# The first query chunk's attention scores as three 32-row products on four row strips

## The chip, the core and the metric

One core of a Trainium2 chip runs the kernel. The metric is device time in microseconds (us), median over executions. The core's engines work side by side: TensorE (PE; the profile shows its matmuls as PE and its weight loads as PEld), VectorE (DVE), ScalarE (ACT), GpSimd (POOL) and SyncE (SP). In this kernel POOL and SP mainly issue DMAs; those of SP are shown as SPq. TensorE writes its results to eight PSUM banks of 128 partitions by 512 fp32 values, from which ACT and DVE read.

## The reference

The output puts two results side by side: multi-query attention (A) of one `x`, and a two-dimensional Fourier filter (B) of another.

```python
# A: S = 2048, D = 448, H = 16 heads of 28, one key and one value head
q = (x @ wq).reshape(B, S, H, Dh).transpose(0, 2, 1, 3)
k, v = x @ wk, x @ wv
scores = einsum("bhqd,bkd->bhqk", q, k) * (Dh ** -0.5)
p = softmax(scores, axis=-1)
a = einsum("bhqk,bkd->bhqd", p, v).transpose(0, 2, 1, 3).reshape(B, S, H * Dh) @ wo
# B
y = irfft2(rfft2(x2) * (w_r + 1j * w_i), s=(S, D))
return concatenate([a, y], axis=-1)
```

## The kernel before, in words

**First part.** `x` is projected to queries, keys and values in fp32r (each operand split into a high part h and a low part l, three products hh + hl + lh). Beside this run the first transforms of B, all but the last of eight blocks. The order here is made by `Plan`: tasks with engines, durations and due times, put in order greedily. Queries lie in `qraw`: group g (four heads) and query chunk c (512 queries) make a 128 x 512 block, each head in a 32-row strip (28 values, then 4 rows that another use fills). The queries are masked and an upper bound for the scores is added in the spare rows (`cvec`), so that the exponential needs no maximum. A number `bits`, read by all engines, decides whether a rare branch (`tc.If`, L616) is taken; it is not taken here.

**Main part.** 256 steps: for c in 4 chunks, g in 4 groups, kc in 16 blocks of 128 keys. A step has:

- four scores (L1124), one for each head: a product of 128 rows, weights `ka[:, 128 keys]`, moving `qa[c, g][:, head]`. The 128 rows hold the key parts kh, kh, kl, kl in four strips and the query parts qh, ql, qh, ql, so that one product gives (kh + kl)(qh + ql). Each goes to one of banks 0 to 6;
- four exponentials on ACT (L1141), bank to `p` in SBUF, which free the bank;
- values (L1156): four 32-column products in fp32, one for each head, added up over the 16 key blocks of a group in bank 7. The profile counts each as two matmuls.

`build_q` makes `qa` of a group while the group before runs: three DVE operations (L195 to L197), then nine DMAs on SP (L206, L207) that put the head strips of qh and ql into the four strips of one of two slots. For the first group, L604, L606 and `twice` (L188) do the same with ACT and DVE copies at the end of the first part. `keys_cast`, `keys_low` and `keys_strip` (L484) make `ka`: the first half of the keys in the first part, the second half at the start of the main part.

After a group, `group_out` (L1001) copies bank 7 out, and it is normalised through POOL DMAs. After a chunk, 12 "w" units multiply by the output weights (`woh`, `wol`; L1044), and the last stages of B ("z" units L946, L972) fill TensorE too. `wo_load` and `wo_split` (L760, L763, L765) load and split the output weights. B's middle transforms run on DVE behind everything else.

**What sets the order.** The main part is written out by a planner. It keeps a clock for each engine (`clk`) with assumed costs and chooses on TensorE between scores, values and fill units; DVE work is queued by planned time (`after`, `background`). Every engine then executes its own list in order; the planned times never reach the chip. `size()` gives the steps of one batch of values: two, or four when enough fill work is there, so that TensorE changes between 128-row products and 32-column ones once in two or four steps. Fill units are allowed only where `work` holds them; in the first chunk there are none but one piece of B (`first_fill`).

Of the kernel before, what the change touches and what calls it, by code (L numbers as in the profile page):

```python
# [32 lines left out]
LEAD = 7  # L33
WARM = 8, 8
FIRST = 8
PLACES = (3, 5, 6, 8, 9, 10)


# [57 lines left out]
def kernel(ctx: ExitStack, tc: tile.TileContext, t: dict):  # L96
# [87 lines left out]

    qa, slots = {}, []

    def twice(u, q, *_):
        return nc.vector.tensor_copy(q[64:128, 2 * u:2 * u + 2], q[0:64, 2 * u:2 * u + 2].bitcast(F32))  # L188

    def build_q(c, g, first=False):  # L190
        cs = slice(c * CW, (c + 1) * CW)
        qt = qp.tile([128, CW], F32, name="qt")
        qh = qp.tile([128, CW], F32R, name="qh")
        ql = qp.tile([128, CW], F32R, name="ql")
        nc.vector.tensor_scalar(qt, qraw[:, g, cs], mask, cvec[:, g, c:c + 1], op0=ALU.mult, op1=ALU.add)  # L195
        nc.vector.tensor_copy(qh, qt)
        nc.vector.tensor_tensor(ql, qt, qh.bitcast(F32), op=ALU.subtract)  # L197
# [4 lines left out]
        if first:  # L202
            return q, qh, ql
# [8 lines left out]
    with tc.tile_pool(name="f1", bufs=2) as f1[0], tc.tile_pool(name="w1", bufs=1) as w1, ExitStack() as ctx1:  # L212
# [257 lines left out]
        kls, hi_ = {}, {}  # L470

        def keys_cast(h, eng):
            hs = slice(h * 1024, h * 1024 + 1024)
            cast(eng, lambda: ka[:32, hs], lambda: kf[:32, hs])

        def keys_low(h):
            hs = slice(h * 1024, h * 1024 + 1024)
            kls[h] = w1.tile([32, 1024], F32R, name="kl")
            low(lambda: kls[h], lambda: kf[:32, hs], lambda: ka[:32, hs])

        def keys_strip(h, p):
            hs = slice(h * 1024, h * 1024 + 1024)
            src = ka[0:32, hs] if p == 1 else kls[h]
            nc.sync.dma_start(ka[32 * p:32 * p + 32, hs].bitcast(F32), src.bitcast(F32))  # L484

        halves = slice(0, 1024), slice(1024, 2048)

# [33 lines left out]
        slots.append(qp.tile([128, 4, CW], F32R, name="qa0", bufs=1))  # L521
        qa[0, 0] = slots[0]

        for c in range(1, NC):
            for g in range(NG):
# [21 lines left out]
                if c == 2 and g == 3:  # L547
                    fetch("v", range(7, 14), slice(0, 1536), POOL, *(evacs[a, b] for a in range(3) for b in (1, 2, 3)))
                    kc = add(ACT, 1.0, lambda: keys_cast(0, ACT), krow_[0], *fetched["k0"])
                    kl = add(DVE, 1.1, lambda: keys_low(0), kc)  # L550
                    for p in (1, 2, 3):
                        add(SP, 0.55, lambda p=p: keys_strip(0, p), kl, kb=128)
# [45 lines left out]
        tv = add(PE, 1.05, turn_values, users[-6], ident_, *krow_, *fetched["v"])  # L598
        users.append(add(ACT, 0.6, lambda: nc.scalar.activation(vs, pvs[0], AF.Copy), tv))
        fm_task(L, True)  # L600
        cq = []
        for i in range(4):
            r = slice(32 * i, 32 * i + 32)
            cq.append([add(ACT, 0.6, lambda i=i, r=r: nc.scalar.activation(slots[0][32:64, i], q3[2][r].bitcast(F32), AF.Copy),  # L604
                           qd, due=56.0 + i),
                       add(DVE, 0.41, lambda i=i, r=r: nc.vector.tensor_copy(slots[0][0:32, i], q3[1][r].bitcast(F32)),  # L606
                           qd, due=56.0 + i)])
# [8 lines left out]
        with tc.If(rv > int(np.float32(BOUND).view(np.int32))), tc.tile_pool(name="g1", bufs=1) as g1:  # L616
# [24 lines left out]
            nc.vector.memset(cvec, 0.0)  # L641
            nc.vector.memset(mask, 1.0)
            parts = build_q(0, 0, True)
            q, qh, ql = parts
            for i in range(4):
                for p, src in enumerate((qh, ql)):
                    nc.vector.tensor_copy(q[32 * p:32 * p + 32, i], src[32 * i:32 * i + 32].bitcast(F32))
            for u in range(2):
                twice(u, q)


        fft1_out(L, pb6)
# [36 lines left out]
    def wide(n):  # L689
        return 0.165 + 0.00107 * n  # L690

    woh = ap.tile([128, 7, D], F32R, name="woh", bufs=1)
    wol = ap.tile([128, NG, D], F32R, name="wol", bufs=1)
    csh = ap.tile([128, 4, 128], F32R, name="csh", bufs=1)
    csl = ap.tile([128, 4, 128], F32R, name="csl", bufs=1)

# [63 lines left out]
        nc.gpsimd.dma_start(wo[g], t["wo"][:, g])  # L760

    def wo_split(g):
        V.tensor_copy(woh[:, g], wo[g])  # L763
        if g < NG:
            TT(wol[:, g], wo[g], woh[:, g].bitcast(F32), op=ALU.subtract)  # L765


    t1v = t1.rearrange("(r k) l u (n f) -> r (k l u) n f", r=2, f=113)
# [269 lines left out]
    def wo_mm(p, c, k, gs):  # L1038
        s = slice(k * 128, k * 128 + 128)
        for g in gs:  # L1040
            spare = c < NC - 1
            for n, (x, w, m) in enumerate(((oh, woh, g), (oh, wol, g), (ol, woh, g + 3 * spare))):
                if n < 2 or g or not spare:
                    mm(p, x[c][:, g, s], w[:, m], start=(g == 0 and n == 0), stop=(g == NG - 1 and n == 2))  # L1044

    def wo_out(p, c, k):
        y = ap.tile([128, D], F32, name="ya")
# [72 lines left out]
    def score(i):  # L1120
# [12 lines left out]
        if kc == 0 and h == 0 and n + 1 < len(order):  # L1133
            after(clk["pe"] + 3.0, 1.7, build_q, *order[n + 1])

    def exps():

        while waiting and waiting[0][0] < 4 * done_steps + P_BUFS:
            i, b, at = waiting.popleft()
            p = pt[i] = pp.tile([128, CW], F32, name="p")  # L1140
            nc.scalar.activation(p, bank[b], AF.Exp, scale=SCALE)  # L1141
# [45 lines left out]
    sc, bt, begun, since, gap = 0, 0, False, 0, 2  # L1187
    parts, tail = deque((k, g) for k in range(4) for g in range(NG - 1)), {}

    def partial():  # L1190
# [19 lines left out]
        return max(1.8, n * (total - done[0]) / max(250 - done_steps, 3)) if n > 2 else 0.0  # L1210

    done_steps, quota = 0, 0.0
    n = size()
    while done_steps < 256:
        if begun:
            vector(clk["pe"])
# [5 lines left out]
        if not begun and not soon:  # L1222
            first_fill()
            begun = True
        elif t_v <= clk["pe"] + 0.05 and (sc >= min(need + LEAD, 1024) or not soon):
            values(done_steps, n)
            done_steps += n
            exps()
# [171 lines left out]
```

## Time and profile before

| | |
|---|---|
| median of 3 runs | 634.85 us (634.68 to 637.08) |
| profiled execution | 635.8 us, its span 633.1 us |
| first score starts | 70.33 us |
| first exponential starts | 70.83 us |
| ACT in the stretch 71.43 to 196.52 us (chunk 0) | busy all of it, with 257 exponentials, the two cut by its ends counted |
| granted TensorE clock | 1.000 over the span |

Times in the rows are from the start of the span. A row of a timeline has start, length, engine, line, operation, output <- input, how many are merged, and in brackets how long the engine was idle before and what ended that. A matmul's length is from its start to its modelled end, so lengths of neighbours overlap; the pace is read from starts.

### The profile page before, as it was taken

The numbers are of one execution on the slowest core, as the hardware profiler recorded it, in microseconds if no ns is written. First come the engines' busy times: TensorE is split into PE (matmuls) and PEld (weight loads), VectorE is DVE, ScalarE is ACT, GpSimd is POOL, SyncE is SP. The second block draws the span as 40 slices with busy tenths as digits, with TensorE's granted clock in tenths as the row PEclk, the third lists the DMA queues.
The fourth block names the chain that finished last, engine by engine and source line by source line (L and its number), as shares of the span: only waits on it lengthen the run. The fifth ranks groups of instructions, "written<-read, shape, count | busy, mean of one in ns | idle before, by whom it ended". The sixth has DMA issues, their size and how long they took to land.

```text
span 633.1 us, 11646 instructions
## 1 busy us (share of the span) xinstructions
PE 626.6 (99%) x4336; PEld 351.5 (56%) x4336; DVE 347.3 (55%) x693; ACT 546.5 (86%) x1100; POOL 90.5 (14%) x167
## 2 busy tenths in 40 slices
PE   9999999999999999999999999999999999999997
PEld 7877544444444446554446656657564446564445
DVE  6999624979796988897632713236562201330104
ACT  4644899999999998789998788878779998879991
POOL 1021140102121101020223011021110101020200
PEclk9999999999999999999999999999999999999999
DMA  8766587031243231131763432251523121140002
GB/s 297 249 181 159 141 244 235 16 84 45 66 130 89 75 83 31 61 83 26 223 211 97 128 84 76 64 145 65 163 83 68 31 67 31 36 110 2 16 1 87
DMA packets 30738, 64.62 MB, mean 102 GB/s; under 512 B 7105, under 2 KB 16673, under 8 KB 29717
## 3 DMA queue, kind: packets, MB, share of 16 engines
q1 hardware_dynamic: 22714, 42.33, 23.8%
q0 software_dynamic: 7536, 20.98, 11.2%
q8 instruction: 34, 0.56, 0.4%
q10 hardware_dynamic: 432, 0.57, 0.2%
q14 instruction: 22, 0.18, 0.1%
HBM read 30.58 MB, written 16.30 MB: 74 GB/s over the span
## 4 chain that ended last, share of the span: by engine, by line
PE 88%; ACT 0%; issue 0%; DVE 0%; ACTq 0%
PE b L1124 41%; PE b L1156 37%; PE b L1044 5%; PE b L946 2%; PE b L972 2%; PE b L1277 0%; PE b L162 0%; ACT yb L1059 0%; DVE yb L1062 0%; ACTq L1060 0%
## 5 line engine op out<-in xcount | busy, mean ns | idle before, releaser
L1141 ACT ACTIVATE p<-b 128x512 f32<-128x512 f32 x1024 | 506.3, 769 | 40.9 <-PE b L1156 28.7
L1124 PE MATMUL b<-qa,ka 128*128 128x512 f32 x1024 | 282.7, 408 | 0.4 <-PEq L616 0.4
L1124 PEld LDWEIGHTS b<-qa,ka 128*128 128x128 f32 x1024 | 181.8, 188 | 127.8 <-ACT p L1141 86.0
L1156 PE MATMUL b<-p,vs 128*32 128x512 f32 x2048 | 241.5, 597 | 0.0
L1156 PEld LDWEIGHTS b<-p,vs 128*32 128x32 f32 x2048 | 55.8, 109 | 122.5 <-issue 120.4
L1001 DVE COPY qraw<-b 128x512 f32<-128x512 f32 x15 | 10.4, 692 | 86.6 <-PE b L1156 86.6
L1006 POOL DMA_DIRECT2D sd<-qraw x15 | 8.9, 595 | 264.9 <-DVE qraw L1001 253.3
L1048 DVE COPY ya<-b 128x448 f32<-128x448 f32 x12 | 7.5, 625 | 65.2 <-PE b L1044 47.4
L829 DVE SCALAR_TENSOR_TENSOR X<-w,X 128x226 f32<-128x226 f32 (+2 forms) x72 | 34.0, 473 | 2.4
L1014 POOL DMA_DIRECT2D R<-rd x60 | 30.4, 513 | 30.1 <-DMA rd<-rs 30.1
L978 DVE COPY w<-b 128x256 f32<-128x256 f32 x16 | 6.8, 424 | 36.6 <-PE b L972 35.0
L320 ACT ACTIVATE qraw<-b 128x512 f32<-128x512 f32 x16 | 9.4, 598 | 18.5 <-PE b L316 18.4
L316 PE MATMUL b<-xh,wqh 128*128 128x512 f32 x64 | 23.7, 401 | 0.4 <-DVE xh L264 0.4
L316 PE MATMUL b<-xh,wql 128*128 128x512 f32 x64 | 23.0, 389 | 0.0
L1044 PE MATMUL b<-woh,oh 128*128 128x448 f32 x60 | 21.9, 365 | 0.0
L1044 PE MATMUL b<-wol,oh 128*128 128x448 f32 x60 | 21.8, 363 | 0.0
L954 DVE CAST zh<-b 113x512 fp32r<-113x512 f32 (+1 forms) x16 | 11.0, 689 | 16.5 <-ACT p L1141 11.0
L822 DVE SCALAR_TENSOR_TENSOR w<-X 128x113 f32<-128x113 f32 (+2 forms) x56 | 17.7, 353 | 0.1
L1044 PE MATMUL b<-woh,ol 128*128 128x448 f32 x48 | 17.5, 364 | 0.0
L316 PE MATMUL b<-xl,wqh 128*128 128x512 f32 x48 | 17.3, 390 | 0.0
L1022 DVE TENSOR_TENSOR qraw<-qraw,R 128x512 f32<-128x512 f32 x15 | 10.3, 685 | 12.5 <-DMA R<-rd 12.5
L865 DVE TENSOR_TENSOR w<-X,wf 128x904 f32<-128x904 f32 x16 | 17.0, 1097 | 0.3
(120 smaller groups left out, 534.4 us busy)
## 6 DMA issues: line engine op xcount, KB each, us to landing
qa<-qa SPq DMA_DIRECT2D x15, 512.0 KB
xb<-xb SPq DMA_DIRECT2D x8, 512.0 KB
ob<-yo SPq DMA_DIRECT2D x16, 256.0 KB
qa<-qh SPq DMA_DIRECT2D x60, 64.0 KB
qa<-ql SPq DMA_DIRECT2D x60, 64.0 KB
t<-bs SPq DMA_DIRECT2D x16, 226.0 KB
X<-t POOLq DMA_DIRECT2D x8, 452.0 KB, 10.3
wf<-w POOLq DMA_DIRECT2D x8, 452.0 KB, 3.8
```

The costliest lines, as they stand in the source:

```text
L316: mm(pq[c, g], w[:, j, gs], x[:, j], start=(j == 0 and n == 0), stop=(j == 3 and n == 1))
L822: STT(out, y, sy, x, op0=ALU.mult, op1=ALU.add if c > 0 else ALU.subtract)
L829: todo(226 * n, lambda d=d, q=q: STT(both(d), t[0].rearrange("p r n f -> p r (n f)"), q, both(a), op0=ALU.mult, op1=ALU.add))
L865: TT(u[r], both(s), wt[k][:, r:r + 1].to_broadcast([128, 2, 452]), op=ALU.mult)
L946: mm(pz[:w, j], fb["c2", q % 2][:, e, j, :w], fb["fi", q % 2][:, j], start=True, stop=True)
L954: V.tensor_copy(h, pz)
L972: mm(py[:, k], c[:w, kind], z, start=(n == 0), stop=(n == 2))
L1014: nc.gpsimd.dma_start(R[32 * i:32 * i + DH], rd[i:i + 1].to_broadcast([DH, CW]))
L1044: mm(p, x[c][:, g, s], w[:, m], start=(g == 0 and n == 0), stop=(g == NG - 1 and n == 2))
L1124: mm(bank[b], ka[:, kc * 128:(kc + 1) * 128], qa[c, g][:, h], start=True, stop=True)
L1141: nc.scalar.activation(p, bank[b], AF.Exp, scale=SCALE)
L1156: mm(bank[7][32 * i:32 * i + 32], vs[:, kc], pt.pop(4 * st + i), start=(kc == 0), stop=(kc == 15))
```

## The change

For the first chunk (64 steps, `STRIPS = 4` groups) a step's scores are made by three rounds of four 32-row products: round one kh times qh, round two kh times ql, round three kl times qh, each round with the four heads on the four row strips and into four different banks, added up there. So queries stay in the layout in which `build_q` makes them (`qh`, `ql` whole), and for this chunk the copies into slots go away: L604, L606 and L188 for the first group, nine SP DMAs each for groups 1 to 3. The keys are kept as two tiles, kh and kl, each copied into all four strips (six DMAs for half the keys, where there were three). The product kl times ql, which the 128-row form has, is left out in this chunk.

The first chunk is no longer written by the choosing loop but by a fixed one: scores of step k, then values of step k - 2, a batch of one step. From step 64 on the old loop runs with `ka` in the old layout, which four DMAs (`old_keys`) fill from kh and kl. The output weights `woh`, `wol` take the memory of kh and kl (`tag="keys"`) and are loaded and split later: planned at 126 + 4.5 g, before at 11 + 6 g for the first four and 66 + 6 g for the other three.

```diff
-    ka = cp.tile([128, S], F32R, name="ka")
+    keys = cp.tile([128, 11 * D], F32R, name="keys", tag="keys")
+    kh, kl = keys[:, :S], keys[:, S:2 * S]
...
+    def build_q(c, g):
         n = 4 * c + g
-        if len(slots) <= n < 2:
-            slots.append((qp if n == 0 else ap).tile([128, 4, CW], F32R, name=f"qa{n}", bufs=1))
+        qt = qp.tile([128, CW], F32, name="qt")
+        if n < STRIPS and n % 2:
+            qh, ql = (slots[n // 2][:, p] for p in range(2))
+        else:
+            qh = qp.tile([128, CW], F32R, name="qh")
+            ql = qp.tile([128, CW], F32R, name="ql")
+        split_q(qt, qh, ql, c, g)
+        if n < STRIPS:
+            qa[c, g] = qh, ql
+            return
         q = qa[c, g] = slots[n % 2]
...
         def keys_strip(h, p):
             hs = slice(h * 1024, h * 1024 + 1024)
-            src = ka[0:32, hs] if p == 1 else kls[h]
-            nc.sync.dma_start(ka[32 * p:32 * p + 32, hs].bitcast(F32), src.bitcast(F32))
+            for k in (kh, kl):
+                nc.sync.dma_start(k[32 * p:32 * p + 32, hs].bitcast(F32), k[0:32, hs].bitcast(F32))
...
-        cq = []
-        for i in range(4):
-            r = slice(32 * i, 32 * i + 32)
-            cq.append([add(ACT, 0.6, lambda i=i, r=r: nc.scalar.activation(slots[0][32:64, i], q3[2][r].bitcast(F32), AF.Copy),
-                           qd, due=56.0 + i),
-                       add(DVE, 0.41, lambda i=i, r=r: nc.vector.tensor_copy(slots[0][0:32, i], q3[1][r].bitcast(F32)),
-                           qd, due=56.0 + i)])
-        for u in range(2):
-            add(DVE, 0.61, lambda u=u: twice(u, slots[0]), *cq[2 * u], *cq[2 * u + 1], bt_)
...
     def wo_split(g):
-        V.tensor_copy(woh[:, g], wo[g])
+        if g == 0:
+            both = cp.tile([128, 11, D], F32R, name="both", tag="keys")
+            woh.extend(both[:, n] for n in range(7))
+            wol.extend(both[:, n] for n in range(7, 11))
+        V.tensor_copy(woh[g], wo[g])
         if g < NG:
-            TT(wol[:, g], wo[g], woh[:, g].bitcast(F32), op=ALU.subtract)
+            TT(wol[g], wo[g], woh[g].bitcast(F32), op=ALU.subtract)
+
+    def old_keys():
+        for p, k in enumerate((kh, kh, kl, kl)):
+            r = slice(32 * p, 32 * p + 32)
+            nc.sync.dma_start(ka[r].bitcast(F32), k[r].bitcast(F32))
...
+    def strips(st):
+        c, g, kc = steps[st]
+        bs = heapq.nsmallest(4, range(7), key=free.__getitem__)
+        qh, ql = qa[c, g]
+        for n, (k, q) in enumerate(((kh, qh), (kh, ql), (kl, qh))):
+            for i in range(4):
+                r = slice(32 * i, 32 * i + 32)
+                mm(bank[bs[i]], k[r, kc * 128:(kc + 1) * 128], q[r], start=(n == 0), stop=(n == 2))
...
-    w0 = 5.0 if FIRST == 8 else 28.0
+    after(12.0, 0.0, old_keys)
     for g in range(7):
-        at = w0 + 6 * g if g < NG else 60.0 + 6 * g
-        after(at, 0.0, wo_load, g)
-        after(at + 6.0, 1.1, wo_split, g)
+        at = 126.0 + 4.5 * g
+        after(at - 4.0, 0.0, wo_load, g)
+        after(at, 1.1, wo_split, g)
...
+    for k in range(16 * STRIPS):
+        if k:
+            vector(clk["pe"])
+        strips(k)
+        if k == 1:
+            first_fill()
+        if k > 1:
+            values(done_steps, 1)
+            done_steps += 1
+            exps()
```

How the order changes on TensorE inside the first chunk. Before, two steps of values, then eight scores; `b_83` is bank 7, the other `b_` are banks 0 to 6, and "waits Activation" means that the bank must first be freed by an exponential:

```order
L1156 MATMUL b_83<-p,vs 32x512 x8
L1124 MATMUL b_79<-qa_127,ka 128x512 [waits Activation_49]
L1124 MATMUL b_77<-qa_127,ka 128x512 [waits Activation_49]
L1124 MATMUL b_78<-qa_127,ka 128x512 [waits Activation_49]
L1124 MATMUL b_80<-qa_127,ka 128x512 [waits Activation_49]
L1124 MATMUL b_81<-qa_127,ka 128x512 [waits Activation_49]
L1124 MATMUL b_82<-qa_127,ka 128x512 [waits Activation_49]
L1124 MATMUL b_76<-qa_127,ka 128x512 [waits Activation_49]
```

(the eighth score, again to `b_79`, and the next values follow). Now, with L1138 the line of the strips and L1173 that of the values, on the same engine and in the same part:

```order
L1173 MATMUL b_83<-p,vs 32x512 x4
L1138 MATMUL b_81<-qh,keys 128x512 [waits Activation_49]
L1138 MATMUL b_79<-qh,keys 128x512 [waits Activation_49]
L1138 MATMUL b_76<-qh,keys 128x512 [waits Activation_49]
L1138 MATMUL b_80<-qh,keys 128x512 [waits Activation_49]
L1138 MATMUL b_81<-ql,keys 128x512
L1138 MATMUL b_79<-ql,keys 128x512
L1138 MATMUL b_76<-ql,keys 128x512
L1138 MATMUL b_80<-ql,keys 128x512
```

(round three, with kl, again names qh and keys and follows; then the next values). Eight 128-row products and a change of form in two steps became 24 of 32 rows and two changes, and all waits for banks stand in the first round.

On ACT, the end of the first part before; `al` is a result of B's last block, `vs` the values' weights, and `bits` the branch:

```order
L604 ACTIVATE qa_127<-ql 32x512 [waits DVE_49]
L604 ACTIVATE qa_127<-ql 32x512 x3
L415 ACTIVATE al<-b_80 128x452 [waits PE_49]
L415 ACTIVATE al<-b_76 128x452 [waits PE_49]
L599 ACTIVATE vs<-b_78 128x512 [waits PE_49]
L615 TENSOR_LOAD bits [waits DVE_49]
```

Now:

```order
L178 ACTIVATE bs<-b_83 128x2x2x113 [waits PE_49]
L419 ACTIVATE al<-b_80 128x452 [waits PE_49]
L419 ACTIVATE al<-b_76 128x452 [waits DVE_49,PE_49]
L599 ACTIVATE vs<-b_78 128x512 [waits PE_49]
L606 TENSOR_LOAD bits [waits DVE_49]
```

The four copies ahead of `al` are gone. On DVE, around the end of the first chunk, before (`qt`, `qh`, `ql`: `build_q` of the second chunk's second group; L1001: `group_out` of the first chunk's last):

```order
L195 TENSOR_SCALAR qt<-qraw,mask,cvec 128x512
L196 CAST qh<-qt 128x512 [waits DMAHW4_49,DMAHW2_49,DMAHW6_49,DMAHW0_49,DVE_49]
L197 TENSOR_TENSOR ql<-qt,qh 128x512 [waits DMAHW5_49,DMAHW3_49,DMAHW7_49,DMAHW1_49,DVE_49]
L1001 COPY qraw<-b_83 128x512 [waits PE_49]
L824 SCALAR_TENSOR_TENSOR w<-X 128x113
```

Now, with L996 the `group_out`:

```order
L191 TENSOR_SCALAR qt<-qraw,mask,cvec 128x512
L192 CAST qh<-qt 128x512 [waits DMAHW5_49,DMAHW3_49,DMAHW7_49,DMAHW1_49,DVE_49]
L193 TENSOR_TENSOR ql<-qt,qh 128x512 [waits DMAHW4_49,DMAHW2_49,DMAHW6_49,DMAHW0_49,DVE_49]
L753 CAST both<-wo 128x448 [waits DMASW1_49,PE_49]
L755 TENSOR_TENSOR both<-wo,both 128x448 [waits DVE_49]
L996 COPY qraw<-b_83 128x512 [waits PE_49]
L860 TENSOR_TENSOR w<-X,wf 128x904
```

The first split of the output weights stands between them now, and waits for TensorE: the last strips must have read the keys whose memory it takes. The other six follow within the next 45 rows.

More of the change, by code (lines that the diff above doesn't have):

```diff
@@ L35 @@
 FIRST = 8
+STRIPS = 4
 PLACES = (3, 5, 6, 8, 9, 10)
@@ L185, with split_q @@
     qa, slots = {}, []
-    def twice(u, q, *_):
-        return nc.vector.tensor_copy(q[64:128, 2 * u:2 * u + 2], q[0:64, 2 * u:2 * u + 2].bitcast(F32))
-    def build_q(c, g, first=False):
+    def split_q(qt, qh, ql, c, g):
         cs = slice(c * CW, (c + 1) * CW)
-        qt = qp.tile([128, CW], F32, name="qt")
-        qh = qp.tile([128, CW], F32R, name="qh")
-        ql = qp.tile([128, CW], F32R, name="ql")
         nc.vector.tensor_scalar(qt, qraw[:, g, cs], mask, cvec[:, g, c:c + 1], op0=ALU.mult, op1=ALU.add)
@@ L549 @@
                     kc = add(ACT, 1.0, lambda: keys_cast(0, ACT), krow_[0], *fetched["k0"])
-                    kl = add(DVE, 1.1, lambda: keys_low(0), kc)
+                    kd = add(DVE, 1.1, lambda: keys_low(0), kc)
                     for p in (1, 2, 3):
-                        add(SP, 0.55, lambda p=p: keys_strip(0, p), kl, kb=128)
+                        add(SP, 1.1, lambda p=p: keys_strip(0, p), kd, kb=256)
                 if c == 3 and g == 2:
@@ L642 @@
             nc.vector.memset(mask, 1.0)
[L643 to L649, printed above, removed]
+            split_q(*q3, 0, 0)
         fft1_out(L, pb6)
@@ L690, in wide @@
         return 0.165 + 0.00107 * n
-    woh = ap.tile([128, 7, D], F32R, name="woh", bufs=1)
-    wol = ap.tile([128, NG, D], F32R, name="wol", bufs=1)
+    ka = ap.tile([128, S], F32R, name="ka", bufs=1)
+    slots += [ap.tile([128, 4, CW], F32R, name=f"qa{n}", bufs=1) for n in range(2)]
+    woh, wol = [], []
     csh = ap.tile([128, 4, 128], F32R, name="csh", bufs=1)
@@ L1043, in wo_mm @@
                 if n < 2 or g or not spare:
-                    mm(p, x[c][:, g, s], w[:, m], start=(g == 0 and n == 0), stop=(g == NG - 1 and n == 2))
+                    mm(p, x[c][:, g, s], w[m], start=(g == 0 and n == 0), stop=(g == NG - 1 and n == 2))
     def wo_out(p, c, k):
@@ L1134, in score @@
             after(clk["pe"] + 3.0, 1.7, build_q, *order[n + 1])
+    def strips(st):
[6 more added lines that the diff above has]
+                mm(bank[bs[i]], k[r, kc * 128:(kc + 1) * 128], q[r], start=(n == 0), stop=(n == 2))
+        switch("r")
+        if clk["new"]:
+            clk["pe"] += 0.105
+        at = clk["pe"]
+        for i, b in enumerate(bs):
+            at = max(at + 0.005, free[b])
+            free[b] = inf
+            waiting.append((4 * st + i, b, at + 3 * 0.23 + 0.31))
+        clk["pe"] = at + 3 * 0.23
+        clk["new"] = False
+        exps()
+        if kc == 0:
+            after(clk["pe"] + 3.0, 1.7, build_q, *order[4 * c + g + 1])
     def exps():
@@ L1185 @@
         after(6.0 + 9.0 * (q - FIRST), 1.35, late_fold, q, 0)
-    sc, bt, begun, since, gap = 0, 0, False, 0, 2
+    sc, since, gap = 64 * STRIPS, 0, 2
     parts, tail = deque((k, g) for k in range(4) for g in range(NG - 1)), {}
@@ L1212 @@
     done_steps, quota = 0, 0.0
+    for k in range(16 * STRIPS):
[7 more added lines that the diff above has]
+            done_steps += 1
+            exps()
     n = size()
     while done_steps < 256:
-        if begun:
-            vector(clk["pe"])
+        vector(clk["pe"])
         hold()
@@ L1221 @@
         more = sc < 1024
[L1222 to L1225, printed above, removed]
+        if t_v <= clk["pe"] + 0.05 and (sc >= min(need + LEAD, 1024) or not soon):
             values(done_steps, n)
```

11 lines of the change are left out of this document (3 added, 8 removed).

## The prediction

> **What bounds the kernel now.** I read the page's engines and slices first, then the groups, then ACT's busy time chunk by chunk, then the timeline of TensorE inside the first chunk.
>
> ```profile
> PE 626.6 (99%) x4336; PEld 351.5 (56%) x4336; DVE 347.3 (55%) x693; ACT 546.5 (86%) x1100; POOL 90.5 (14%) x167
> ...
> ACT  4644899999999998789998788878779998879991
> ...
> PE 88%; ACT 0%; issue 0%; DVE 0%; ACTq 0%
> PE b L1124 41%; PE b L1156 37%; PE b L1044 5%; PE b L946 2%; PE b L972 2%; PE b L1277 0%; PE b L162 0%; ACT yb L1059 0%; DVE yb L1062 0%; ACTq L1060 0%
> ```
>
> TensorE looks like the bound: 99% busy, 88% of the chain, 41% of it in the scores. But a matmul's length overlaps its neighbour's, so "busy" doesn't say that TensorE has no room, and the slices show ACT at 9 just where the change acts. The next view settles that stage. It takes the exponentials (L1141) alone, in four stretches that each hold one chunk.
>
> ```profile
> 71.43:196.52 125.09, 125.09 (x257) 1.00 0.44 120
> 196.52:329.00 132.48, 125.75 (x258) 1.00 0.35 99
> 329.00:481.00 152.00, 127.07 (x256) 1.00 0.34 97
> 481.00:616.00 135.00, 126.85 (x258) 1.00 0.17 42
> ```
>
> Columns: stretch, its length, ACT's busy time (instructions). 256 exponentials keep ACT busy for 125 to 127 us in every chunk. The later chunks last longer, since TensorE has fill work there. The first lasts exactly as long as ACT is busy: 125.09 / 256 = 0.489 us each, 1.955 us for a step of four, without a gap. Is 0.489 ACT's own pace, or does TensorE set it? An activation of 452 columns gives an answer from outside the main part:
>
> ```profile
> 68.31 0.99 ACT L415 ACTIVATE al<-b 128x452 f32<-128x452 f32 x2
> ...
> L415 ACT ACTIVATE a<-b 128x452 f32<-128x452 f32 x14 | 7.6, 547 | 4.2 <-PE b L152 4.2
> ...
> L1141 ACT ACTIVATE p<-b x1024: 590/672/1151, 70.8 to 616.3; 128x512 f32<-128x512 f32 x171
> ```
>
> Two back to back take 0.99 us and one 0.547, so the second comes 0.443 us after the first. The shortest exponential is 0.590 - 0.547 = 0.043 us longer, for its 60 more columns; so I estimate 0.486 us for ACT alone. The measured 0.489 is that pace. ACT holds the first chunk and could gain at most 256 x 0.003 = 0.8 us.
>
> **Scores and values in the first chunk.** How much faster does TensorE become?
>
> ```profile
> 132.29 2.13 PE L1124 MATMUL b<-qa,ka 128*128 128x512 f32 x8
> 134.36 1.92 PE L1156 MATMUL b<-p,vs 128*32 128x512 f32 x16
> 136.21 2.13 PE L1124 MATMUL b<-qa,ka 128*128 128x512 f32 x8
> ...
> 138.27 1.92 PE L1156 MATMUL b<-p,vs 128*32 128x512 f32 x16
> ...
> 77.30 2.36 PE L1124 MATMUL b<-qa,ka 128*128 128x512 f32 x9
> ...
> 338.40 3.64 PE L1156 MATMUL b<-p,vs 128*32 128x512 f32 x32
> ...
> 59.56 0.39 PE L316 MATMUL b<-xl,wqh 128*128 128x512 f32 x1
> ...
> 60.46 0.39 PE L316 MATMUL b<-xh,wql 128*128 128x512 f32 x1
> ```
>
> - Now: values start at 134.36 and again at 138.27, so two steps take 3.91 us, 1.955 a step. TensorE and ACT are within the reading error of each other.
> - A score: nine take 2.36 us, eight 2.13: 0.23 each. From 136.21 to 138.27 are 2.06 us: 8 x 0.23 = 1.84, and 0.22 for filling the array and changing the form.
> - Values: 32 matmuls take 3.64 us and 16 take 1.92: (3.64 - 1.92) / 4 = 0.43 for a round of four. From 134.36 to 136.21 are 1.85 us, four rounds, 1.72, and 0.13 for the change back. One step alone has two rounds: 0.86 + 0.13 = 0.99.
> - A strip round isn't in the trace. The nearest row is an fp32r product of the same 512 columns with new weights each time: (60.46 - 59.56) / 4 = 0.226. If four strips run side by side, a round takes that, and the strips of a step 3 x 0.226 + 0.22 = 0.90 instead of 4 x 0.23 + 0.11 = 1.03.
>
> A step with strips so takes 0.90 + 0.99 = 1.89 us on TensorE, 0.065 less than now: of the 0.24 saved on products 0.175 goes to the extra change of form. ACT still needs 1.955, so these 64 x 0.065 = 4 us become TensorE waiting at the first round for banks. The first chunk takes 125 us again: cost and gain 0.
>
> What must not be exceeded: the room of 0.065 us is 0.022 a round, so TensorE takes over the bound at a round of 0.248, and from there each 0.01 us costs 3 x 64 x 0.01 = 1.9 us. Can four banks at a time starve ACT though TensorE has room? Seven banks rotate, so step k + 1's fourth strip waits for the first exponential of step k. From its end to the next step's first finished score are three rounds, 0.68, and a matmul's tail, about 0.2 (0.39 long, 0.226 apart); ACT meanwhile has three more exponentials, 1.47 us. No.
>
> For the round's bounds, the rows with several tiles of the array at once:
>
> ```profile
> 71.42 0.59 PEld L162 LDWEIGHTS b<-al,fwl 64*64 64x64 f32 x16 [0.37 <-issue]
> 71.43 0.99 PE L162 MATMUL b<-al,fwl 64*64 64x226 f32 x16
> ...
> 66.17 0.74 PEld L152 LDWEIGHTS b<-cs,f 113*32 113x32 f32 x32
> 66.17 0.99 PE L152 MATMUL b<-cs,f 113*32 113x113 f32 x32
> ...
> L162 PE MATMUL b<-a,fw 64*64 64x226 f32 x112 | 7.1, 364 | 0.0
> L152 PE MATMUL b<-cs,f 113*32 113x113 f32 x512 | 14.3, 261 | 0.0
> ```
>
> L162 has two row halves by two column halves: 16 matmuls of 0.364 us in 0.99 us, four rounds, (0.99 - 0.36) / 3 = 0.21 apart. One after the other they would be 16 x 0.21 = 3.4 us. So row halves do overlap, weights included. From below nothing suggests a round under 0.226. From above: suppose weight loads of different tiles take turns, hidden in those rounds. Then a load of 64 columns takes at most 0.21 / 4 = 0.052 us, one of 32 (L152: (0.99 - 0.26) / 7 / 4) 0.026; both give 0.104 for the strips' 128 columns, 0.42 for four. The round lies between 0.226 and 0.42. I take 0.226, since both tiled rows show no sign of turns.
>
> **The rest of the change.**
>
> ```profile
> 65.69 2.59 ACT L604 ACTIVATE qa<-ql 32x512 fp32r<-32x512 f32 x4
> ...
> 65.84 0.39 PE L495 MATMUL b<-prod,blk 128*128 128x12 f32 x2 [0.33 <-DVE prod L489]
> ...
> 67.67 1.15 PE L597 MATMUL b<-ident,kf 32*128 32x32 f32 x16 [0.23 <-ACT qa L604]
> 67.67 1.33 DVE L188 CAST qa<-qa 64x1024 fp32r<-64x1024 f32 x2
> ...
> 68.75 1.14 PE L162 MATMUL b<-a,fw 64*64 64x226 f32 x16
> ...
> 70.33 0.94 PE L1124 MATMUL b<-qa,ka 128*128 128x512 f32 x3 [0.44 <-PEq L616]
> 70.83 0.60 ACT L1141 ACTIVATE p<-b 128x512 f32<-128x512 f32 x1 [1.05 <-PE b L1124]
> ```
>
> - First part: 2.59 us of copies on ACT and 1.33 + 1.7 on DVE go. Ahead of the first score TensorE waits there for 0.33 (DVE) and 0.23 (ACT); the transposes of the values (L597), B's matmuls (L162) and the branch follow one another on TensorE whatever ACT does. Gain 0.3 to 0.56 us. Against it, the first exponential comes after three rounds instead of one product, 2 x 0.226 = 0.45 later. Taken together: 0 to 0.3 later, I take 0.15.
> - SP: nine DMA issues less for each of three groups, nothing on TensorE waits for SP there. Six key DMAs instead of three, about 0.6 us each on SP (row below), put the last stores of B's first stage 1.8 us later in either half; behind them come the loads of X. The cover: DVE touches X only after the first `group_out`, which waits 8.54 us for TensorE at 105.04. The second half of the keys is needed at step 8, 70.3 + 8 x 1.955 = 86; its six DMAs are issued by about 73 + 6 x 0.6 = 77. `old_keys` is needed at 196.
>
> ```profile
> 73.44 1.18 SPq L484 DMA_DIRECT2D ka<-kl  x2
> ...
> 105.04 0.69 DVE L1001 COPY qraw<-b 128x512 f32<-128x512 f32 x1 [8.54 <-PE b L1156]
> ...
> 81.31 0.39 DVE L763 CAST woh<-wo 128x448 fp32r<-128x448 f32 x1 [5.82 <-DMA wo<-wo]
> 81.74 0.63 DVE L765 TENSOR_TENSOR wol<-wo,woh 128x448 fp32r<-128x448 f32 x1
> ...
> 192.94 0.69 DVE L197 TENSOR_TENSOR ql<-qt,qh 128x512 fp32r<-128x512 f32 x1
> 199.00 0.69 DVE L1001 COPY qraw<-b 128x512 f32<-128x512 f32 x1 [5.37 <-PE b L1156]
> ...
> 230.36 0.69 DVE L1001 COPY qraw<-b 128x512 f32<-128x512 f32 x1 [3.01 <-PE b L1156]
> ```
>
> - Output weights: four splits of 0.39 + 0.63 = 1.02 us move from DVE's idle stretch at 80 to behind 193.6. The first waits for the last strips, about 196, and is done at 197; what is queued behind it, `group_out`, waits for TensorE until 199.00 anyway. The other three, 3.1 us, push B's transforms back and meet a wait of 3.01 us at 230.36. The first z unit comes one batch later (after step 136's scores instead of 132's); 23 batches of four remain 23, and the last fill still lies 28 steps before the end. POOL's loads of the weights now stand behind those of X, which start earlier. Cost 0; if the cover fails, 3 us of DVE delay a filling that has this much room.
>
> **The sum** is 635.8 + 0.15 + 0 + 0 = 635.95 for the profiled execution, whose time is its span of 633.1 and 2.7 around it. It lies 0.95 above the median, so I forecast 634.85 + 0.15 = **635.0 us**.
>
> **The rivals.**
>
> - *TensorE becomes the bound, by strips that overlap only partly* (slower). It decides from a round of 0.248 us. For it: the room is only 10% of a round, and a step has eight more weight loads than now. Against it: L162 shows full overlap. At 0.28 the loss is 0.032 x 192 = 6.1 us, 641; at 0.31, 12 us, 647. The Trainium skill ("TensorE: Matmul & The Clock Gate", section "Part 3: Packing small matmuls") states 3.07 times the speed for four 32-row tiles at 512 columns. By that figure a round would take 4 x 0.226 / 3.07 = 0.294, an estimate, and the kernel 644; no run here shows it yet.
> - *Weight loads of four strips take turns* (slower): a round of up to 0.42, (0.42 - 0.248) x 192 = 33 us, up to 668; half-way 651. Against it: only bounds, no row, allow it.
> - *No overlap at all*: 12 x 0.226 = 2.71 for the products, 2.71 + 0.22 + 0.99 - 1.955 = 1.97 more a step, 126 us. L162 speaks against it.
> - *Faster*: the whole 2.59 us of L604 was on the path, and ACT reaches 0.486. Less 0.45 that is 2.9 us, 632. Against it: TensorE's own chain ahead of 70.33.
>
> **How the numbers follow.** 0.5%, 3.2 us, is about what a measurement of this kernel can tell from no change. ACT stays the bound: 0.52, giving 633 to 637. Partial overlap 0.28: up to 638 (a round up to 0.265) within 0.5% with 0.05 of it, the rest slower. Turns 0.10, no overlap 0.02, both slower. The faster case 0.08: half of it I leave within 0.5%, the rest covers what I don't see. So faster 0.06, same 0.57, slower 0.37. The range from 632.5 to 648 takes the first case, the second up to a round of 0.315 and part of the last, some 0.8; the likeliest case alone has 633 to 637.
>
> **What would show it.** Right: ACT has again no idle time between 71 and 196 us, its stretch for 256 exponentials again takes 125 us, and TensorE's first-round loads wait for `p`. The second rival shows as steps over 1.96 us, ACT idle in each, released by L1138; by the distance of L1138's starts from round to round one reads the round. Wrong weights' timing would show as DVE or TensorE waiting for `both` after 196 us, a longer first part as a first strip after 70.4 us.

## The result, and the profile after

The changed kernel takes 640.69 us (median of 5 runs, 639.84 to 641.30), the kernel before beside it 635.62 us (5 runs, 634.68 to 637.08): a ratio of 1.0077, with a 95% interval of 1.0056 to 1.0098. The time lies in the range forecast, 5.7 us above the value, and on the slower side of the 0.5% bound. The profiled execution took 640.69 us as well; its span is 638.9 us, 5.8 more than before.

The page of the changed kernel: engines, one line of the slices, the chain by engine, and one group.

```profile
PE 628.9 (98%) x4848; PEld 341.6 (53%) x4848; DVE 343.6 (54%) x687; ACT 543.8 (85%) x1096; POOL 90.7 (14%) x167
...
PEclk9999999999999989999999999999999999999999
...
PE 77%; DVE 6%; DMA 3%; issue 2%; POOL 1%; ACT 0%; ACTq 0%; DVEq 0%; POOLq 0%
...
L1173 PE MATMUL b<-p,vs 128*32 128x512 f32 x2048 | 249.6, 602 | 4.0 <-DVE qraw L996 3.8
```

Three lines differ from before. The chain, which held TensorE alone, now has DVE with 6%, DMA with 3% and POOL with 1%. The clock has one slice of 8 (224 to 240 us). The values' products (L1173) waited 3.8 us for DVE's `group_out` (L996), where before no such wait stood:

```profile
L1156 PE MATMUL b<-p,vs 128*32 128x512 f32 x2048 | 241.5, 597 | 0.0
```

All of it lies behind the first chunk. The first chunk itself, in the view by stretches, ACT's exponentials (L1158) alone:

```profile
70.75:196.09 125.34, 125.09 (x257) 1.00 0.31 94
196.09:337.00 140.91, 128.56 (x263) 0.98 0.35 103
```

The first chunk lasts 125.34 us (125.09 before), with ACT busy for 125.09 of it, the same as before. What got longer is the second row. The stretch of the same work in both kernels, from shortly behind the first chunk to the `group_out` of the second chunk's second group, all engines (before, then after):

```profile
197.00:269.00 72.00, 72.00 (x441) 37.89 (x441) 60.66 (x101) 67.00 (x138) 9.03 (x17) 1.00 0.25 66
```

```profile
196.60:274.50 77.90, 74.12 (x441) 38.62 (x441) 57.81 (x98) 67.22 (x137) 12.22 (x23) 0.96 0.29 82
```

441 matmuls each, 72.00 us before and 77.90 after: 5.9 us, the whole loss. TensorE was idle for 77.90 - 74.12 = 3.78 us of it, and its clock averaged 0.96. DVE was busy for less time than before (57.81 against 60.66), so DVE isn't late by work; it waited. Its timeline, the splits of the output weights (L753, L755) and `group_out` (L996) only; in brackets the idle time before the instruction and what ended it:

```profile
195.08 0.39 DVE L753 CAST both<-wo 128x448 fp32r<-128x448 f32 x1
195.50 0.62 DVE L755 TENSOR_TENSOR both<-wo,both 128x448 fp32r<-128x448 f32 x1
198.57 0.69 DVE L996 COPY qraw<-b 128x512 f32<-128x512 f32 x1 [2.45 <-PE b L1173]
207.16 0.39 DVE L753 CAST both<-wo 128x448 fp32r<-128x448 f32 x1 [6.23 <-DMA wo<-wo]
...
223.49 0.39 DVE L753 CAST both<-wo 128x448 fp32r<-128x448 f32 x1 [4.72 <-DMA wo<-wo]
...
234.96 0.69 DVE L996 COPY qraw<-b 128x512 f32<-128x512 f32 x1
```

The first split goes as forecast. The second waits 6.23 us and the fifth 4.72 us for their weights to arrive, and since DVE works in order, everything behind them comes later, `group_out` too: it stood at 230.36 before, with 3.01 us to spare, and stands at 234.96 with nothing to spare. Why are the weights late? POOL's timeline, which issues their loads (L746):

```profile
187.75 0.54 POOL L746 DMA_DIRECT2D wo<-wo  x1
199.55 0.59 POOL L1001 DMA_DIRECT2D sd<-qraw  x1 [11.26 <-DVE qraw L996]
201.63 0.56 POOL L1002 DMA_DIRECT2D rs<-sd  x1 [1.49 <-DMA sd<-qraw]
202.19 0.54 POOL L746 DMA_DIRECT2D wo<-wo  x1
...
214.63 0.54 POOL L852 DMA_DIRECT2D wf<-w  x1 [5.58 <-DVE w L860]
215.45 0.55 POOL L1007 DMA_DIRECT2D rd<-rs  x1 [0.29 <-DVE both L753]
218.49 2.02 POOL L1009 DMA_DIRECT2D R<-rd  x4 [2.50 <-DMA rd<-rs]
220.50 1.09 POOL L746 DMA_DIRECT2D wo<-wo  x2
```

The second load stands on POOL behind the issue of `sd`, which waits 11.26 us for the `group_out` of the first chunk's last group, and behind `rs`, which waits for `sd`. So it is issued at 202.19, though POOL had nothing to do from 188.3 on. The weights are there at 207.16, 5.0 us after the issue. The two loads of 220.50 stand in the same way behind `R`, which waits for `rd`, and both behind the issue of `wf`, which waits 5.58 us for DVE. Memory isn't what held them back: `wo` has two buffers, the second load takes one that no load has used yet, and the fifth takes the third's, whose split was done at 211.88. And TensorE:

```profile
229.79 2.14 PE L1119 MATMUL b<-qa,ka 128*128 128x512 f32 x8
235.70 3.64 PE L1173 MATMUL b<-p,vs 128*32 128x512 f32 x16 [3.78 <-DVE qraw L996]
239.28 2.78 PE L1119 MATMUL b<-qa,ka 128*128 128x512 f32 x8
241.98 1.92 PE L1173 MATMUL b<-p,vs 128*32 128x512 f32 x16
```

The values of steps 80 and 81 need the bank that `group_out` empties. They start at 235.70 after an idle time of 3.78 us, and then take 3.64 us for sixteen products that usually take 1.92. From step 80 to step 82 are 241.98 - 235.70 = 6.28 us, where the kernel before takes 236.21 - 232.29 = 3.92, without a wait:

```profile
232.29 1.92 PE L1156 MATMUL b<-p,vs 128*32 128x512 f32 x16
...
236.21 1.92 PE L1156 MATMUL b<-p,vs 128*32 128x512 f32 x16
```

That is another 2.36 us. The clock column (the one ahead of the last two) of the view by stretches gives the reason:

```profile
230.00:234.00 4.00, 1.93 (x8) 1.21 (x7) 3.83 (x9) 4.00 (x10) 0.00 (x0) 0.99 0.06 17
234.00:236.00 2.00, 0.30 (x4) 0.20 (x8) 1.97 (x4) 0.80 (x2) 0.06 (x1) 0.50 0.18 57
236.00:240.00 4.00, 4.00 (x18) 1.02 (x11) 3.93 (x6) 0.00 (x0) 1.09 (x2) 0.50 0.39 98
240.00:244.00 4.00, 4.00 (x25) 1.89 (x24) 4.00 (x4) 3.89 (x8) 0.00 (x0) 0.91 0.36 85
```

In the trace's record of the clock it is halved from 233.93 to 240.76 us, 6.83 us. Waiting 3.78 and slow products 2.36 make 6.14, of the 5.9 us that the stretch is longer.

### The profile page after: what moved, and what is told of

The parts are those of the page before. It is cut to its first block, busy times and chain, and to the rows that moved or that the text cites. A ratio compares the mean times of both kernels' runs of the same rounds, so it can differ in the third digit from the quotient of the medians.

```text
span 638.9 us, 12853 instructions
## 1 busy us (share of the span) xinstructions
PE 628.9 (98%) x4848; PEld 341.6 (53%) x4848; DVE 343.6 (54%) x687; ACT 543.8 (85%) x1096; POOL 90.7 (14%) x167
## 4 chain that ended last, share of the span: by engine, by line
PE 77%; DVE 6%; DMA 3%; issue 2%; POOL 1%; ACT 0%; ACTq 0%; DVEq 0%; POOLq 0%
PE b L1173 33%; PE b L1119 27%; PE b L1138 7%; PE b L1039 5%; PE b L941 2%; DVE w L860 2%; PE b L967 2%; DVE X L824 1%; DMA wo<-wo 1%; DVE X L866 1%; DMA X<-t 1%; DMA rd<-rs 0%; DVE w L817 0%; PE b L1300 0%; DMA sd<-qraw 0%
## 5 line engine op out<-in xcount | busy, mean ns | idle before, releaser
L1158 ACT ACTIVATE p<-b 128x512 f32<-128x512 f32 x1024 | 505.9, 757 | 49.0 <-PE b L1173 34.3
L1173 PE MATMUL b<-p,vs 128*32 128x512 f32 x2048 | 249.6, 602 | 4.0 <-DVE qraw L996 3.8
L1119 PE MATMUL b<-qa,ka 128*128 128x512 f32 x768 | 215.0, 408 | 0.0
L1119 PEld LDWEIGHTS b<-qa,ka 128*128 128x128 f32 x768 | 136.6, 189 | 90.4 <-ACT p L1158 50.3
L1173 PEld LDWEIGHTS b<-p,vs 128*32 128x32 f32 x2048 | 52.8, 109 | 123.1 <-issue 115.2
L1001 POOL DMA_DIRECT2D sd<-qraw x15 | 9.0, 600 | 251.5 <-DVE qraw L996 251.5
L996 DVE COPY qraw<-b 128x512 f32<-128x512 f32 x15 | 10.4, 691 | 62.7 <-PE b L1173 62.7
L1039 PE MATMUL b<-both,oh 128*128 128x448 f32 x120 | 33.9, 364 | 0.0
L1138 PE MATMUL b<-qh,keys 32*128 32x512 f32 x256 | 32.9, 443 | 0.8 <-ACT p L1158 0.5
L1138 PEld LDWEIGHTS b<-qa,keys 32*128 32x128 f32 x384 | 19.2, 183 | 26.8 <-ACT p L1158 26.8
L1138 PE MATMUL b<-qa,keys 32*128 32x512 f32 x384 | 33.1, 425 | 0.0
L1138 PEld LDWEIGHTS b<-qh,keys 32*128 32x128 f32 x256 | 16.1, 182 | 26.9 <-ACT p L1158 25.8
L1039 PEld LDWEIGHTS b<-both,oh 128*128 128x128 f32 x120 | 22.5, 188 | 5.0 <-issue 0.8
```

The source lines that it names most:

```text
L1039: mm(p, x[c][:, g, s], w[m], start=(g == 0 and n == 0), stop=(g == NG - 1 and n == 2))
L1119: mm(bank[b], ka[:, kc * 128:(kc + 1) * 128], qa[c, g][:, h], start=True, stop=True)
L1138: mm(bank[bs[i]], k[r, kc * 128:(kc + 1) * 128], q[r], start=(n == 0), stop=(n == 2))
L1173: mm(bank[7][32 * i:32 * i + 32], vs[:, kc], pt.pop(4 * st + i), start=(kc == 0), stop=(kc == 15))
```

## The experiments

The theory that the traces give: the late loads of the output weights, behind POOL's waiting issues, make the loss, and the strips have no part in it. The rivals: the splits' own 3.1 us on DVE make it; the strips make it, by TensorE's pace in the first chunk or by what follows from it.

**Late weights alone, in the kernel before.** The weights keep memory of their own, only the times at which loads and splits are due change:

```diff
-        at = w0 + 6 * g if g < NG else 60.0 + 6 * g
-        after(at, 0.0, wo_load, g)
-        after(at + 6.0, 1.1, wo_split, g)
+        at = 126.0 + 4.5 * g
+        after(at - 4.0, 0.0, wo_load, g)
+        after(at, 1.1, wo_split, g)
```

> The kernel before, with one part of the change alone: the output weights are loaded and split at the late planned times, in their own memory; scores, keys and first part stay. Theory (the loss comes from the late output weights: VectorE waits for their loads, TensorE then for VectorE's copy out of bank 7): 4 to 6 us slower than before, 639.5 to 641.5, with TensorE idle 2 to 4 us behind the copy out of the second chunk's first group, and a halved clock there. Rival (the strips, the one-step batches or the keys' new memory cost it): within 1 us of before.

637.71 us (10 runs) against 636.54 for the kernel before beside it (21 runs): 1.0018 (1.0005 to 1.0032). A miss in size: some 1.2 us, not 4 to 6. The rows of POOL, then of DVE, say why:

```profile
188.70 0.54 POOL L760 DMA_DIRECT2D wo<-wo  x1
196.30 0.72 POOL L760 DMA_DIRECT2D wo<-wo  x1
201.81 0.65 POOL L1006 DMA_DIRECT2D sd<-qraw  x1 [4.79 <-DVE qraw L1001]
```

```profile
209.02 0.39 DVE L763 CAST woh<-wo 128x448 fp32r<-128x448 f32 x1 [3.30 <-DMA wo<-wo]
...
232.19 0.69 DVE L1001 COPY qraw<-b 128x512 f32<-128x512 f32 x1 [1.26 <-PE b L1156]
```

Here the planner's order put two loads ahead of `sd` instead of one. DVE waits for weights 3.30 and 1.22 us instead of 6.23 and 4.72, `group_out` still has 1.26 us to spare, and TensorE doesn't wait for it. The same splits, as late, cost nearly nothing when the second weight is there. That was not yet the same place on POOL's list as in the changed kernel, so it was made so:

**The same with each load due 1 us ahead of its split, not 4.** The one edit against the last kernel:

```diff
-        after(at - 4.0, 0.0, wo_load, g)
+        after(at - 1.0, 0.0, wo_load, g)
```

> The kernel before with late output weights as in the first run of this study, but the loads planned 1 us ahead of the splits instead of 4, so that GpSimd's list has the second load behind the issues of the first chunk's last group, as the changed kernel has it. Theory (the place on GpSimd's list, not the strips): VectorE waits 5 us or more at the second split, and the kernel loses 3 to 6 us, 639 to 642. Rival (it takes the strips too): as that first run, 1 us over before.

648.64 us (4 runs) against 636.46 (14 runs): 1.0173 (1.0141 to 1.0204). The direction as the theory has it, the size above it. Now the second load stands behind `sd` and `rs`, at 204.73, and TensorE waits for `group_out`:

```profile
242.96 3.64 PE L1156 MATMUL b<-p,vs 128*32 128x512 f32 x16 [8.54 <-DVE qraw L1001]
```

DVE waited three times (6.95, 3.89 and 4.78 us), since a later load was behind as well. The clock was halved for 10.24 us, and from step 80 to step 82 are 249.37 - 242.96 = 6.41 us, 2.49 over the usual. Wait and slow products make 11.0 of the 12.2 us. (In this execution the clock was halved for another 3.41 us at 70.78, where the first part ends.) No strip is in this kernel: the loss needs none, only the loads' place.

**The changed kernel with all seven weights loaded early.** The splits stay where they are; the raw weights go into memory that is free until the second chunk (that of `oh` and `ol`):

```diff
-        wo[g] = ap.tile([128, D], F32, name="wo", tag="ya")
+        if g % NG == 0:
+            raw = ap.tile([128, NG * CW], F32, name="wraw", tag=("oh", "ol")[g // NG])
+            for n in range(g, min(g + NG, 7)):
+                wo[n] = raw[:, (n - g) * D:(n - g + 1) * D]
...
-        after(at - 4.0, 0.0, wo_load, g)
+        after(36.0, 0.0, wo_load, g)
```

> The changed kernel, with the raw output weights loaded early (planned at 36, all seven) into buffers that oh and ol use later; the splits stay at their late places. Theory (the waits for the loads are the loss, not the splits' own 7 us and not the strips): the two waits of 6.2 and 4.7 us on VectorE are gone, TensorE no longer waits for bank 7, 634 to 636, that is 0 to 0.7 us under before. Rival one (the splits' work in that stretch is enough to hold VectorE up): 637 to 639. Rival two (strips): as the changed kernel, 640 to 641.

635.39 us (11 runs) against 636.54 for the kernel before (21 runs): 0.9982 (0.9973 to 0.9991), the fastest of the kernels that leave no work out. DVE:

```profile
200.56 0.39 DVE L756 CAST both<-wraw 128x448 fp32r<-128x448 f32 x1
...
229.65 0.69 DVE L999 COPY qraw<-b 128x512 f32<-128x512 f32 x1 [6.01 <-PE b L1176]
```

No split waits, and `group_out` has 6.01 us to spare. Strips and late splits are all still there (the seven splits take 5.2 us, not the 7 of the expectation), so neither makes the loss. The 0.18% below the kernel before is no gain of the strips as far as the record shows: 13 of the 21 executions of the kernel before had a granted clock of 0.994 to 0.997 over the whole and a median of 636.75 us; the other 8, at 1.000, have 635.64. The 11 here were all at 0.998 or more.

**Only the first two loads early.** Loads 0 and 1 due at 100, the other five as in the change:

```diff
-        after(at - 4.0, 0.0, wo_load, g)
+        after(100.0 if g < 2 else at - 4.0, 0.0, wo_load, g)
```

> The changed kernel, with the first two of the seven output weight loads planned at 100, so that the second stands on GpSimd's list ahead of the issues that wait for the first chunk's last group; the other five and all splits stay. Theory (one load behind those issues is what holds VectorE up first): the wait of 6.2 us at the second split is gone or under 2 us, VectorE reaches the copy out of bank 7 in time or less than 1 us late, 635 to 637. Rival (any late load on GpSimd holds it up alike): 639 or more.

637.19 us (10 runs) against 636.46 (14 runs): 1.0023 (1.0005 to 1.0040). 0.2 us above what was expected, and only partly as thought. The second split no longer waits, but the third takes its place, and the fifth waits as before:

```profile
208.88 0.39 DVE L753 CAST both<-wo 128x448 fp32r<-128x448 f32 x1 [4.40 <-DMA wo<-wo]
...
221.59 0.39 DVE L753 CAST both<-wo 128x448 fp32r<-128x448 f32 x1 [4.77 <-DMA wo<-wo]
```

In the profiled execution (636.45 us) the values of step 80 waited 1.99 us for `group_out`, and the clock stayed full. Four of the ten executions had a granted clock of 0.997 or less over the whole; they took 638.27 to 641.17 us, the six others 636.43 to 637.51. So the first load behind the waiting issues costs 6.23 - 4.40 = 1.8 us less when it is the third. DVE's two waits add up: 9.17 us with 1.99 on TensorE here, 10.95 with 3.78 in the changed kernel, both 1.8 apart.

**Is TensorE faster with strips at all?** In the kernel before, and in the one with early weights, the first chunk's exponentials were halved (256 of 512 columns), so that ACT no longer bounds it; the values read each computed half twice:

```diff
-            nc.scalar.activation(p, bank[b], AF.Exp, scale=SCALE)
+            w = CW // 2 if i < 256 else CW
+            nc.scalar.activation(p[:, :w], bank[b][:, :w], AF.Exp, scale=SCALE)
+            if w < CW:
+                pt[i] = p.rearrange("p (a n) -> p a n", a=2)[:, 0:1].to_broadcast([128, 2, w])
```

> The kernel before, with the first chunk's exponentials over 256 of the 512 columns (the values read these columns twice), so half of the first chunk's exponentials are left out and ScalarE needs some 0.28 us instead of 0.49 for each. It shows TensorE's own pace in the first chunk. Theory (TensorE and ScalarE stand level before): 1.93 to 1.96 us a step, the chunk's stretch 124 to 125.5 us.

> The strips with early loads of the output weights, and the first chunk's exponentials over half the columns as in the run on the kernel before. Theory (strips overlap fully, a round takes 0.226 us): 1.85 to 1.92 us a step, the chunk's stretch 118 to 123 us, 2 to 6 us less than in that run. Rival (strips gain nothing on TensorE and only seem to, since ScalarE hides it): 1.95 us or more.

One execution each, 633.71 and 631.02 us, both with a granted clock of 1.000. TensorE's timeline, first without strips (values of steps 16 and 48 start at 105.98 and 168.58), then with:

```profile
105.98 1.07 PE L1161 MATMUL b<-p,vs 128*32 128x512 f32 x8
...
168.58 0.64 PE L1161 MATMUL b<-p,vs 128*32 128x512 f32 x4
```

```profile
104.41 1.06 PE L1181 MATMUL b<-p,vs 128*32 128x512 f32 x8
105.41 0.98 PE L1141 MATMUL b<-qa,keys 32*128 32x512 f32 x12
106.31 0.64 PE L1181 MATMUL b<-p,vs 128*32 128x512 f32 x4
...
165.13 1.06 PE L1181 MATMUL b<-p,vs 128*32 128x512 f32 x8
```

(168.58 - 105.98) / 32 = 1.956 us a step without strips, (165.13 - 104.41) / 32 = 1.898 with. In a step with strips the values take 1.00 us and the twelve strip products 0.90. So TensorE gains 0.059 us a step, 3.8 us in 64 steps (the chunk's exponentials, first to last, take 124.4 and 121.0 us, 3.4 apart), and in the real kernel ACT's 1.955 covers all of it.

**The share of the halved clock.** Twelve unused products in a free bank ahead of the waiting values of step 80, to keep TensorE busy:

```diff
+    def keep_warm():
+        b = min(range(7), key=free.__getitem__)
+        for _ in range(12):
+            mm(bank[b], ka[:, :128], qa[1, 1][:, 0], start=True, stop=True)
...
+        if o == 80:
+            keep_warm()
```

> The changed kernel with 12 products more on TensorE, into a bank that is free, just ahead of the values that wait for bank 7 in the second chunk; their results are not used. They fill 2.7 us of the wait. Theory (the wait is 3.8 us of the loss, and some 2 us come after it, from the halved clock): the clock stays full, the values after the wait take their usual time, 638 to 639.3, 1.5 to 2.5 us under the changed kernel. Rival (the halved clock has another cause, or costs nothing on the path): 640 to 641.5.

641.54 us (5 runs) against 636.46 (14 runs): 1.0061 (1.0041 to 1.0082). A miss in the median. In the profiled execution (641.70 us) TensorE's wait shrank to 2.05 us, and yet the clock was halved, for 3.41 us instead of 6.83:

```profile
237.56 2.79 PE L1180 MATMUL b<-p,vs 128*32 128x512 f32 x16 [2.05 <-DVE qraw L996]
243.05 1.92 PE L1180 MATMUL b<-p,vs 128*32 128x512 f32 x16
```

Step 80 to 82 took 5.49 us, still 1.57 over the usual; in this execution the second split also waited 7.57 us for its weight. The five executions fall apart by their clock: 638.79 and 639.54 us at 0.999 or more over the whole, near what the theory expected, and 641.54 to 641.87 at 0.996 or 0.997. That agrees with a price of some 2 to 3 us for the halved clock, but four of the five have no record of where their clock fell. With 22 products (`range(22)`) the wait was covered whole:

> The changed kernel with 22 unused products (about 5.0 us) ahead of the values of step 80, in place of 12; DVE's late work is as it was. Theory (the idle time of about 2 us or more halves the clock): TensorE idles under 0.8 us there, the granted clock stays at 0.97 or more in every stretch between 230 and 250 us, and the values of steps 80 and 81 take 3.9 to 4.1 us from step 80's start to step 82's instead of 6.28; the kernel takes 638.5 to 640.0 us, since the products may outlast the wait by up to 1 us. Rival (the clock is halved by something else than the idle time, such as the burst that follows): a stretch with a clock of about 0.5 stays, and the time is 641 to 643 us.

```profile
233.19 5.30 PE L1167 MATMUL b<-qa,ka 128*128 128x512 f32 x22
238.42 1.92 PE L1180 MATMUL b<-p,vs 128*32 128x512 f32 x16
240.28 2.14 PE L1119 MATMUL b<-qa,ka 128*128 128x512 f32 x8
242.34 1.92 PE L1180 MATMUL b<-p,vs 128*32 128x512 f32 x16
```

No idle time, a clock of 1.00 in every stretch from 222 to 248, and 3.92 us from step 80 to 82: as the theory has it in the trace. The time, 640.34 us (5 runs) against 636.45 (7 runs), 1.0055 (1.0039 to 1.0072), is 0.3 above what it expected, and its interval overlaps that of the changed kernel (1.0056 to 1.0098). The profiled execution is the slowest of the five (641.01). In it DVE came to `group_out` 2.25 us later than in the changed kernel (237.21), 1.28 of it since the first chunk ended so much later (197.37 against 196.09), and the products outlasted the wait by about half a microsecond. So the trace shows that the 2.36 us go when the idle time goes; the medians don't tell how much of the loss is the clock's.

## Why the prediction was right and wrong

- **ACT bounds the first chunk at 1.955 us a step: right.** 125.09 us busy of 125.34, and with half the exponential the chunk goes at TensorE's pace. The sign named for it is there too: the strips' weight loads (PEld, L1138) were released by an exponential 65 times, about once a step.
- **A step with strips takes TensorE 1.89 us, 0.90 of it strips: right.** Measured 1.90 and 0.90. The distance of the rounds, in the changed kernel's timeline:

```profile
73.11 0.64 PE L1138 MATMUL b<-qh,keys 32*128 32x512 f32 x4
73.45 0.53 PE L1138 MATMUL b<-ql,keys 32*128 32x512 f32 x4
73.68 0.54 PE L1138 MATMUL b<-qh,keys 32*128 32x512 f32 x4
```

73.45 to 73.68 is 0.23 us, against the 0.226 taken and the 0.248 from which TensorE would bound. (The first interval, 0.34, holds the change of form.) The two rivals of partial overlap and of loads in turns fall with it, though the kernel is slower: a reader who saw only the time might have taken the loss for partial overlap at a round of about 0.28 (641 us).
  The rival that rested on the Trainium skill ("TensorE: Matmul & The Clock Gate", section "Part 3: Packing small matmuls") went by 3.07 times the speed, a round of 0.294; the rows here show about 0.23, nearly four times the speed, and the measurement decides.
- **The first part, 0.15 us later: not seen; if anything it is earlier.** The first exponential starts at 70.16 in this profile (70.83 before). In the six profiles with the new first part it starts between 69.89 and 70.73 us, in the four with the old one between 70.42 and 72.67. The scatter is larger than the term.
- **SP's moved issues, 0: nothing speaks against it.** TensorE's waits between 66 and 200 us are one of 0.45 for a bank, one of 0.4 for the branch and one of 0.22 for DVE; none is for keys or `ka`.
- **Output weights, "Cost 0; if the cover fails, 3 us of DVE delay a filling that has this much room": this step failed.** The part on the first split was right (done at 196.12, and `group_out` still waits 2.45 us for TensorE). For the other three it set their 3.1 us of work against a wait of 3.01 us at 230.36. It left out the last three splits, 0.39 us each, which stood at 159.49 to 169.92 before and now also come ahead of that `group_out`. Still the splits' work was not the price: DVE was busy for less time than before. The price was the waits for loads, 6.23 + 4.72 = 10.95 us, which the step counted at nothing. It named that the loads stand behind those of X, but not that they stand behind `sd`, `rs`, `rd` and `R`, which wait for `group_out` and for one another, and behind `wf`. That POOL had a long wait there was to be read before; its `sd` of this group (the instruction named as the releaser is the one behind `group_out` on DVE) waited 11.57 us:

```profile
199.98 0.59 POOL L1006 DMA_DIRECT2D sd<-qraw  x1 [11.57 <-DVE w L824]
```

And where the cover is gone, the term was not "3 us of DVE" but a wait of TensorE of 3.78 us and 2.36 us of halved clock behind it.
- **The sum.** The span rose by 5.8 us: 0.67 less ahead of the first exponential, 0.25 more in the first chunk, 5.9 in the stretch behind it, and 0.3 elsewhere. (The time around the span was 1.8 us instead of 2.7, so the two profiled executions lie 4.9 us apart.) The 5.9 is what the sum lacks. The slower side was given 0.37, for strips, and came by a way that was no rival. So it is luck that the time lies in the range: its upper part stood there for partly overlapping strips, and these overlap in full. (The chances hold a slip as well: the terms named for no change are 0.52, 0.05 and 0.04, which make 0.61, not 0.57. Nothing else rests on it.) The sign it was to be known by was given: TensorE waiting, and DVE waiting for the weights, after 196 us.

## What to carry to other kernels

A transfer that is moved later has to be placed on the list of the engine that issues it. As the second load here (issued at 202.19), it starts when the last issue ahead of it is released, and if that one waits for the stage's own result, the load comes after the stage instead of before it. A wait of the engine that uses the data covers work of its own, but not a load whose issue hangs on what this engine does next, so such a load belongs ahead of the first waiting issue, as in the version of 635.39 us. And where one engine is busy for the whole of a stage (here ACT, 125.09 of 125.34 us), a faster partner buys only slack: 3.8 us of TensorE time here brought nothing.

## What the runs showed of the hardware

The clock's halved stretches had lengths of 3.413 us (with twelve products), 6.827 (the changed kernel) and 10.24 (late loads due 1 us ahead), one, two and three times the same unit. In the changed kernel the stretch began 2.0 us after TensorE went idle (231.93), while it was still idle, so the slow products came on top of the wait. In the second chunk a gap of 2.05 us was followed by a halved stretch, one of 1.99 us was not. The length of the gap alone doesn't decide: the kernel with 22 products had a halved stretch of 3.413 us at 72 us, where the first part passes into the first chunk and TensorE's gaps are 0.42 and 0.45 us, and the one with loads due 1 us ahead had one at 70.78 behind gaps of 0.83, 0.23 and 0.46; the changed kernel has such gaps there too (0.45 us at 70.81) and kept its clock in the profile shown. What sets the threshold was not tried.

The Trainium skill ("TensorE: Matmul & The Clock Gate", section "Part 1: The HAM clock gate") has the clock watched in windows of 3413 ns that run freely; the lengths here agree with that. Its advice against gaps of more than about 3 us (section "Why this matters for your kernels") would have let the gap of 2.05 us pass; if that gap halved the clock, the advice is too loose for this kernel.
